# Repacking a 448-row contraction into 128-row chunks with paired 64-row tails

## The chip, the core and the metric

The kernel runs on one core of one Trainium2 chip. The metric is device time in microseconds (us) of one execution. A run is labelled fast or slow; with one core, slow only means over 1.5% above the fastest run of the same kernel. Ratios in this text are the mean time of one kernel's fast runs over the mean of the fast runs of the kernel before from the same rounds, so they are not quite the ratio of the medians quoted beside them. Where a ratio is turned into microseconds it is multiplied by 198.5 us, the median time of the kernel before.

PSUM is the memory into which the matmuls of this kernel write; it is addressed in numbered banks. Engine names in the profile lines: PE is TensorE's matmuls, PEld its weight loads, DVE is VectorE, ACT is ScalarE, POOL is GpSimd. L451 is line 451 of that kernel's own source, so line numbers differ between kernels.

## The reference, cut to what matters

```python
B, S, D, H, F = 1, 2048, 448, 16, 1792          # head size 28; all inputs bf16
xn  = layernorm(x)
q, k, v = split_heads(xn @ wqkv)                 # contraction over D = 448
phi(t)  = concat(softmax(t @ w_phi), softmax(-(t @ w_phi)))
kv, z   = sum_s phi(k)^T v, sum_s phi(k)         # linear attention
o       = (phi(q) @ kv) / (phi(q) @ z + 1e-6)
out     = x + o @ wo + silu(xn @ w1) @ w2        # contractions over 448, 448, 1792
```

## The kernel before

D = 448 is no multiple of 128. The kernel before cuts it into four chunks of 112 rows, so every contraction over D is four matmuls that leave 16 of the 128 rows of the array empty.

A small scheduler in the kernel takes operations with named reads and writes. Each operation waits at its head for everything that it needs, and signals once, after its last instruction. An operation that writes two PSUM banks holds and frees both together.

The feed-forward block, its bank alternating between 6 and 7 (`B_PQ`):

```python
def ffn1_block(b):
    tg, k = divmod(b, NK)
    slot = b % 2
    def f(e):
        for c in range(NC_):                      # 4 chunks of 112 rows
            last = e.matmul(bank(B_PQ[slot])[:, :], lhsT=w1_sb[:, c, k * P:(k + 1) * P],
                            rhs=xnT_sb[:, c, tg * TG:(tg + 1) * TG], start=(c == 0), stop=(c == NC_ - 1))
        return last
    sch.add("pe", f, reads=[...], writes=["bank:%d" % B_PQ[slot]], ...)
    sch.add("act", ... Silu from bank(B_PQ[slot]) into hT_sb ...)
```

There are two stages.

```python
for t in range(NT):            # stage one, 16 tiles of 128 positions
    ...                        # layernorm of a later tile (VectorE, GpSimd)
    kv_proj(t)                 # two operations: keys into bank 1 or 2, values into bank 3
    k_exps(t); v_evac(t)       # ScalarE: two exponentials, value eviction
    k_norm(t)                  # VectorE sums and reciprocals, GpSimd product
    q_block(t)                 # one query block of 512 columns, banks 6 and 7 in turn
    xn_transpose(t + LA)       # 4 transposes
    kv_acc(t - 1)              # 8 small matmuls

while ...:                     # stage two, one iteration:
    ffn1_block x 4             # 16 matmuls of 512 columns
    a_mm, a_combine            # attention matmuls, then VectorE
    o_transpose                # 4 transposes
    final_mm, final_out        # 14 + 4 matmuls of 448 columns into bank 3 or 4, then the output
```

The softmax here doesn't subtract the row's maximum and nothing guards it: scores larger than these inputs give would overflow.

## Time and profile before

The median was 198.54 us in three runs.

| | before |
|---|---|
| span of the profiled execution | 197.3 us |
| first feed-forward matmul (end of stage one) | 79.5 us |
| one steady iteration of stage two | 7.51 us |
| 16 feed-forward matmuls of an iteration | 3.46 us |

From the page of the kernel before: the span, the engines' busy time with its share of the span and the number of instructions, then TensorE's busy tenths and the clock that the throttle granted it, in tenths of full speed, in 40 equal slices.

```profile
span 197.3 us, 2897 instructions
PE 174.9 (89%) x1152; PEld 97.2 (49%) x1152; DVE 106.8 (54%) x227; ACT 90.2 (46%) x156; POOL 34.1 (17%) x35
...
PE   0349696996999994999999999999999999999994
...
PEclk9999999999999999699999999999999999999999
```

TensorE is busy without a break in stage two (from slice 16 on) and has gaps in stage one. By this view its clock falls in one slice, just after a gap of 2.5 us at the end of stage one. Stage two begins here:

```profile
79.50 5.11 PE L553 MATMUL ps<-xnT_sb,w_sb 112*128 112x512 bf16 x16
```

One steady iteration, from the timeline of the kernel before (columns: start in us, length in us, engine, line, operation, output and inputs, count, idle time before it and what ended that):

```profile
119.74 2.81 PE L634 MATMUL ps<-w_sb,hT_sb 128*128 128x448 bf16 x14
...
122.39 0.92 PE L637 MATMUL ps<-wo_sb,EqT_sb 112*128 112x448 bf16 x4
...
123.15 3.62 PE L553 MATMUL ps<-xnT_sb,w_sb 112*128 112x512 bf16 x16
...
126.61 0.58 PE L570 MATMUL ps<-rhs_sb,EqT_sb 112*128 112x120 bf16 x8
...
127.03 0.39 PE L612 MATMUL ps<-ident_sb,o_sb 128*112 128x128 bf16 x4
...
127.25 2.81 PE L634 MATMUL ps<-w_sb,hT_sb 128*128 128x448 bf16 x14
```

Read the starts, not the lengths: records of pipelined matmuls overlap. Sixteen feed-forward matmuls go from 123.15 to 126.61, so one every 216 ns. Nothing waits. The next line, of the waits of weight loads (total us, times, longest us), shows how little the Silu evictions hold TensorE up, since one bank is evicted while the other is filled:

```profile
PEld ps L553 <- ACT hT_sb L559: 8.6, 27, 0.4
```

### The profile page before, as it was taken

What the parts mean: (1) busy time and instruction counts of PE and PEld (TensorE: products, weight loads), DVE (VectorE), ACT (ScalarE), POOL (GpSimd) and SP (SyncE); (2) the same over time, 40 slices, a digit from 0 to 9 for tenths busy, and PEclk for the clock granted to TensorE, in tenths of its full rate; (3) what the DMA queues carried; (4) which work ended last, traced back from release to release, by engine and by line L of the source; (5) the groups of instructions that cost most, each with busy time, mean ns of one, the idle gap of its engine ahead of it and who ended that gap; (6) DMA issues with size and microseconds to landing.
All of it is one profiled execution on the core that took longest, in us unless ns stands there. A gap on an engine that the chain in (4) does not pass through costs nothing.

```text
span 197.3 us, 2897 instructions
## 1 busy us (share of the span) xinstructions
PE 174.9 (89%) x1152; PEld 97.2 (49%) x1152; DVE 106.8 (54%) x227; ACT 90.2 (46%) x156; POOL 34.1 (17%) x35
## 2 busy tenths in 40 slices
PE   0349696996999994999999999999999999999994
PEld 0339363553665652455545545445445445555551
DVE  0559796996775452256745345355255255288321
ACT  2308185675778887266524424424415415420200
POOL 3201035545646556000000000000000000000000
PEclk9999999999999999699999999999999999999999
DMA  5938970000000000000000000000000000001001
GB/s 163 331 127 214 283 239 0 0 2 5 0 0 3 0 0 2 0 3 0 0 23 3 23 23 0 28 23 0 23 28 0 23 19 8 23 5 41 27 23 47
DMA packets 9022, 8.70 MB, mean 44 GB/s; under 512 B 880, under 2 KB 8560, under 8 KB 9008
## 3 DMA queue, kind: packets, MB, share of 16 engines
q1 hardware_dynamic: 7616, 7.31, 12.7%
q10 hardware_dynamic: 1392, 1.20, 2.0%
q8 instruction: 9, 0.15, 0.3%
q14 instruction: 5, 0.04, 0.1%
HBM read 6.68 MB, written 1.84 MB: 43 GB/s over the span
## 4 chain that ended last, share of the span: by engine, by line
PE 69%; DVE 3%; POOLq 1%; issue 1%; ACT 1%
PE ps L553 25%; PE ps L634 21%; PE ps L637 6%; PE ps L570 3%; PE ps L443 3%; PE ps L510 3%; PE ps L495 2%; PE ps L451 2%; PE ps L612 2%; DVE xn_sb L409 1%; DVE S_sb L475 1%; POOLq L199 1%; ACT E_sb L461 1%; PE ps L422 1%; DVE R_sb L479 0%
## 5 line engine op out<-in xcount | busy, mean ns | idle before, releaser
L559 ACT ACTIVATE hT_sb<-ps 128x512 bf16<-128x512 f32 x56 | 33.4, 597 | 54.5 <-PE ps L553 54.5
L553 PE MATMUL ps<-xnT_sb,w_sb 112*128 112x512 bf16 x224 | 52.2, 387 | 0.0
L634 PE MATMUL ps<-w_sb,hT_sb 128*128 128x448 bf16 x224 | 45.0, 352 | 0.0
L553 PEld LDWEIGHTS ps<-xnT_sb,w_sb 112*128 112x128 bf16 x224 | 20.0, 100 | 28.3 <-ACT hT_sb L559 8.6
L481 POOL TENSOR_TENSOR phik_sb<-E_sb,R_sb 128x896 bf16<-128x896 f32 x16 | 27.6, 1722 | 28.5 <-DVE R_sb L479 17.7
L634 PEld LDWEIGHTS ps<-w_sb,hT_sb 128*128 128x128 bf16 x224 | 21.3, 98 | 17.9
L583 DVE RECIPROCAL rneg_sb<-ps 128x16 f32<-128x16 f32 x16 | 4.1, 256 | 39.6 <-PE ps L570 39.6
L475 DVE TENSOR_REDUCE S_sb<-E_sb 128x32 f32<-128x896 f32 x16 | 17.3, 1080 | 10.3 <-ACT E_sb L461 10.2
L646 DVE TENSOR_TENSOR y_sb<-ps,x_sb 128x448 bf16<-128x448 f32 x16 | 10.0, 624 | 16.9 <-PE ps L637 16.9
L518 ACT ACTIVATE EqT_sb<-ps 112x512 bf16<-112x512 f32 x32 | 17.4, 594 | 3.4 <-PE ps L510 3.4
L510 PE MATMUL ps<-xnT_sb,wq_sb 112*112 112x512 bf16 x64 | 16.4, 379 | 0.0
L422 PE MATMUL ps<-ident_sb,xn_sb 128*112 128x128 bf16 x64 | 7.5, 261 | 10.1 <-DVE xn_sb L409 9.7
L443 PE MATMUL ps<-wk_sb,xnT_sb 112*128 112x448 bf16 x64 | 15.5, 366 | 0.0
L451 PE MATMUL ps<-wv_sb,xnT_sb 112*128 112x448 bf16 x64 | 15.0, 358 | 0.0
L458 ACT ACTIVATE E_sb<-ps 128x448 f32<-128x448 f32 x16 | 8.7, 544 | 13.3 <-PE ps L443 13.0
L637 PE MATMUL ps<-wo_sb,EqT_sb 112*128 112x448 bf16 x64 | 14.8, 353 | 0.0
L409 DVE TENSOR_SCALAR xn_sb<-x_sb,mv_sb,rstd_sb 128x448 bf16<-128x448 bf16 x16 | 10.4, 667 | 5.3 <-POOL rstd_sb L402 5.3
L619 ACT ACTIVATE EqT_sb<-ps 112x1024 bf16<-112x1024 bf16 x8 | 8.2, 1024 | 11.0 <-PE ps L612 10.8
L422 PEld LDWEIGHTS ps<-ident_sb,xn_sb 128*112 128x112 bf16 x64 | 5.8, 159 | 14.4 <-DVE xn_sb L409 13.9
L391 DVE BATCH_NORM_STATS2 stats_sb<-x_sb 128x6 f32<-128x448 bf16 x16 | 9.6, 597 | 5.6 <-DMA x_sb<-in_A_x_dram 5.6
L495 PE MATMUL ps<-vaug_sb,phik_sb 128*112 128x113 bf16 x128 | 9.7, 218 | 2.5 <-POOL phik_sb L481 2.5
L510 PEld LDWEIGHTS ps<-xnT_sb,wq_sb 112*112 112x112 bf16 x64 | 8.3, 130 | 5.2
(49 smaller groups left out, 160.4 us busy)
## 6 DMA issues: line engine op xcount, KB each, us to landing
w_sb<-in_B_w_dram SPq DMA_DIRECT2D x2, 1568.0 KB, 11.4
x_sb<-in_A_x_dram SPq DMA_DIRECT2D x4, 448.0 KB, 8.1
out_dram<-y_sb SPq DMA_DIRECT2D x16, 112.0 KB, 1.7
hT_sb<-in_A_wqkv_dram ACTq DMA_DIRECT2D x2, 392.0 KB, 6.0
wv_sb<-in_A_wqkv_dram ACTq DMA_DIRECT2D x1, 392.0 KB, 8.4
wo_sb<-in_A_wo_dram SPq DMA_DIRECT2D x1, 392.0 KB, 9.4
wphi_sb<-in_A_w_phi_dram SPq DMA_DIRECT2D x1, 24.5 KB, 5.2
```

The source lines that it names most:

```text
L422: last = e.transpose(out=bank_bf(B_TP)[0:KC, half * 512 + c * P: half * 512 + (c + 1) * P], in_=xn_sb[:, slot, c * KC:(c + 1) * KC], ident ...
L443: last = e.matmul(bank(B_PK[s2])[:, 0:D], lhsT=xnT_sb[:, c, t * P:(t + 1) * P], rhs=wk2_sb[:, c, :], start=(c == 0), stop=(c == NC_ - 1))
L451: last = e.matmul(bank(B_V)[:, 0:D], lhsT=xnT_sb[:, c, t * P:(t + 1) * P], rhs=wv_sb[:, c, :], start=(c == 0), stop=(c == NC_ - 1))
L475: sch.add("dve", lambda e: e.tensor_reduce(out=S_sb[:, s2, :], in_=E_sb[:, s2, :].rearrange("p (g f) -> p g f", f=DH), axis=AX.X, op=ALU.add),
L481: sch.add("pool", lambda e: e.tensor_tensor(out=phik_sb[:, s2, :].rearrange("p (g f) -> p g f", f=DH), in0=E_sb[:, s2, :].rearrange("p (g ...
L495: last = e.matmul(bank(B_KV[sg])[0:KC, j * NV:(j + 1) * NV], lhsT=phik_sb[:, s2, sg * D + j * KC: sg * D + (j + 1) * KC], rhs=vaug_sb[:, s ...
L510: last = e.matmul(bank(B_PQ[slot])[0:KC, :], lhsT=wq2_sb[:, c, j * KC:(j + 1) * KC], rhs=xnT_sb[:, c, tg * TG:(tg + 1) * TG], start=(c == ...
L518: sch.add("act", lambda e, sg=sg: e.activation(out=EqT_sb[:, j, sg, tg * TG:(tg + 1) * TG], in_=bank(B_PQ[slot])[0:KC, :], func=ACTF.Exp, ...
L553: last = e.matmul(bank(B_PQ[slot])[:, :], lhsT=w1_sb[:, c, k * P:(k + 1) * P], rhs=xnT_sb[:, c, tg * TG:(tg + 1) * TG], start=(c == 0), st ...
L559: sch.add("act", lambda e: e.activation(out=hT_sb[:, k, tg * TG:(tg + 1) * TG], in_=bank(B_PQ[slot])[:, :], func=ACTF.Silu), reads=["bank: ...
L634: last = e.matmul(bank(B_ACC[s2])[:, 0:D], lhsT=hT_sb[:, k, t * P:(t + 1) * P], rhs=w2_sb[:, k, :], start=(k == 0), stop=False)
L637: last = e.matmul(bank(B_ACC[s2])[:, 0:D], lhsT=oT_sb[:, c, t * P:(t + 1) * P], rhs=wo_sb[:, c, :], start=False, stop=(c == NC_ - 1))
```

## The change

The intent: cut 448 into three full chunks of 128 rows and a tail of 64. A tail fills half the array's rows, so the tails of two blocks can run at once, one in the upper and one in the lower half. A pair of blocks then takes 3 + 3 + 1 = 7 matmul slots in place of 8. The lower half needs its own copy of the tail rows in partitions 64 to 127, so tail weights are loaded twice, and the tail of every tile is transposed twice, as two 64-column transposes.

The core of the diff (layouts, loads and the query blocks, which are paired in the same way, are cut):

```diff
+        DC = [(0, 128), (128, 128), (256, 128), (384, 64)]
...
+        def tr_chunks(e, src_ap_fn, half):
+            for c in range(NC_):
+                r0, rn = DC[c]
+                outs = [(0, rn)] if c < 3 else [(0, HK), (HK, HK)]     # HK = 64
+                for (po, pn) in outs:
+                    last = e.transpose(out=bank_bf(B_TP)[po:po + pn, ...], in_=src_ap_fn(r0, pn), ...)
...
+        def kv_proj(t):
+            def f(e):
+                mm_full(e, bank(B_PK[s2])[:, 0:D], xl, wkf)            # 3 matmuls of 128 rows
+                mm_full(e, bank(B_V)[:, 0:D], xl, wvf)
+                mm_half(e, bank(B_PK[s2])[:, 0:D], xl, wkf, 0)         # rows 0 to 63
+                return mm_half(e, bank(B_V)[:, 0:D], xl, wvf, HK)      # rows 64 to 127
+            sch.add("pe", f, ..., writes=["bank:%d" % B_PK[s2], "bank:%d" % B_V], ...)
...
-        def ffn1_block(b):
+        def ffn1_pair(b):
+            def f(e):
+                for kk in range(2): mm_full(e, bank(B_PQ[kk])[:, :], ...)
+                for kk in range(2): last = mm_half(e, bank(B_PQ[kk])[:, :], ..., kk * HK)
+                return last
+            sch.add("pe", f, ..., writes=["bank:%d" % B_PQ[0], "bank:%d" % B_PQ[1]], ...)
...
         def final_mm(t):
-                    last = e.matmul(..., lhsT=oT_sb[:, c, ...], rhs=wo_sb[:, c, :], ...)
+                    rn = DC[c][1]
+                    last = e.matmul(..., lhsT=oT_sb[0:rn, c, ...], rhs=wo_sb[0:rn, c, :], ...)
...
-            q_block(t)
+            if t % 2 == 1:
+                q_pair(t - 1)
```

More of the change, by code (lines that the diff above doesn't have):

```diff
@@ L189, in bass_parallel_sum__linear_kernel_hedgehog__dense_activation_silu__prompt_kernel @@
     NA = HPC * (DH + 2)
+    DC = [(0, 128), (128, 128), (256, 128), (384, 64)]
+    HK = 64
     EPS_LN = 1e-5
@@ L206, in bass_parallel_sum__linear_kernel_hedgehog__dense_activation_silu__prompt_kernel @@
         hT_sb = sb("hT_sb", [P, NK, S], BF16)
-        EqT_sb = sb("EqT_sb", [KC, NC_, 2, S], BF16)
+        EqT_sb = sb("EqT_sb", [P, NC_, 2, S], BF16)
         xn_sb = sb("xn_sb", [P, 4, D], BF16)
-        xnT_sb = sb("xnT_sb", [KC, NC_, S], BF16)
-        wv_sb = sb("wv_sb", [KC, NC_, D], BF16)
-        wq2_sb = sb("wq2_sb", [KC, NC_, D], BF16)
-        wk2_sb = sb("wk2_sb", [KC, NC_, D], BF16)
+        xnT_sb = sb("xnT_sb", [P, NC_, S], BF16)
+        wv_sb = sb("wv_sb", [P, NC_, D], BF16)
+        wq2_sb = sb("wq2_sb", [P, NC_, D], BF16)
+        wk2_sb = sb("wk2_sb", [P, NC_, D], BF16)
         wphi_sb = sb("wphi_sb", [KC, NC_, DH], BF16)
@@ L215, in bass_parallel_sum__linear_kernel_hedgehog__dense_activation_silu__prompt_kernel @@
         wbd_sb = sb("wbd_sb", [KC, NC_, HPC, DH], BF16)
-        w1_sb = sb("w1_sb", [KC, NC_, FF], BF16)
+        w1_sb = sb("w1_sb", [P, NC_, FF], BF16)
         w2_sb = sb("w2_sb", [P, NK, D], BF16)
-        wo_sb = sb("wo_sb", [KC, NC_, D], BF16)
+        wo_sb = sb("wo_sb", [P, NC_, D], BF16)
         wqk_sb = hT_sb[0:KC, 0:2, :].rearrange("p a b -> p (a b)")[:, 0:NC_ * 2 * D].rearrange(
@@ L264, in dma, with ld_chunked @@
                     reads=reads, writes=writes, name=name, dma=True, is_out=is_out)
+        def ld_chunked(q, dst, src, reads, res, name):
+            dma(q, dst[:, 0:3, :], src[0:384, :].rearrange("(c p) n -> p c n", p=P),
+                reads=reads, writes=[res + ":a"], name=name + "a")
+            dma(q, dst[0:HK, 3, :], src[384:448, :], reads=reads, writes=[res + ":b"], name=name + "b")
+            dma(q, dst[HK:P, 3, :], src[384:448, :], reads=reads, writes=[res + ":c"], name=name + "c")
         for g in range(4):
@@ L280, in bass_parallel_sum__linear_kernel_hedgehog__dense_activation_silu__prompt_kernel @@
             if g == 2:
-                dma("act", wv_sb[:, :, :],
-                    A_wqkv[:, 2 * D:3 * D].rearrange("(c p) n -> p c n", p=KC),
-                    reads=[], writes=["wv"], name="ld_wv")
+                ld_chunked("act", wv_sb, A_wqkv[:, 2 * D:3 * D], [], "wv", "ld_wv")
         def late_loads():
             gate = ["xnT:2"]
-            dma("sp", w1_sb[:, :, :], B_w1.rearrange("(c p) n -> p c n", p=KC),
-                reads=gate, writes=["w1"], name="ld_w1")
-            dma("sp", wo_sb[:, :, :], A_wo.rearrange("(c p) n -> p c n", p=KC),
-                reads=gate, writes=["wo"], name="ld_wo")
+            ld_chunked("sp", w1_sb, B_w1, gate, "w1", "ld_w1")
+            ld_chunked("sp", wo_sb, A_wo, gate, "wo", "ld_wo")
             dma("sp", w2_sb[:, :, :], B_w2.rearrange("(k p) n -> p k n", p=P),
@@ L364, in fold @@
                         last = None
-                        for c in range(NC_):
-                            last = e.matmul(
-                                bank(bk)[0:KC, c * KC:(c + 1) * KC],
-                                lhsT=wT_sb[:, qk * NC_ + c, i * KC:(i + 1) * KC],
-                                rhs=wbd_sb[:, c, :, :].rearrange("p a b -> p (a b)"),
-                                start=True, stop=True)
+                        r0, rn = DC[i]
+                        outs = [(0, rn)] if i < 3 else [(0, HK), (HK, HK)]
+                        for (po, pn) in outs:
+                            for c in range(NC_):
+                                last = e.matmul(
+                                    bank(bk)[po:po + pn, c * KC:(c + 1) * KC],
+                                    lhsT=wT_sb[:, qk * NC_ + c, r0:r0 + pn],
+                                    rhs=wbd_sb[:, c, :, :].rearrange("p a b -> p (a b)"),
+                                    start=True, stop=True)
                         return last
@@ L375, in emit_wprep_fold @@
                     dst = (wq2_sb if qk == 0 else wk2_sb)[:, i, :]
-                    src = bank(bk)[0:KC, 0:D]
+                    src = bank(bk)[:, 0:D]
                     if qk == 1 or i % 2 == 0:
@@ L414, in ln_apply @@
                 name="xn%d" % t)
+        def tr_chunks(e, src_ap_fn, half):
+            last = None
+            for c in range(NC_):
+                r0, rn = DC[c]
+                outs = [(0, rn)] if c < 3 else [(0, HK), (HK, HK)]
+                for (po, pn) in outs:
+                    last = e.transpose(
+                        out=bank_bf(B_TP)[po:po + pn, half * 512 + c * P: half * 512 + (c + 1) * P],
+                        in_=src_ap_fn(r0, pn), identity=ident_sb[:, :])
+            return last
         def xn_transpose(t):
@@ L418, in xn_transpose @@
             half = t % 2
-            def f(e):
-                last = None
-                for c in range(NC_):
-                    last = e.transpose(
-                        out=bank_bf(B_TP)[0:KC, half * 512 + c * P: half * 512 + (c + 1) * P],
-                        in_=xn_sb[:, slot, c * KC:(c + 1) * KC],
-                        identity=ident_sb[:, :])
-                return last
-            sch.add("pe", f, reads=["xn:%d" % slot, "ident"], writes=["tp:%d" % half],
-                    name="xnT_tr%d" % t)
+            sch.add("pe", lambda e: tr_chunks(e, lambda r0, rn: xn_sb[:, slot, r0:r0 + rn], half),
+                    reads=["xn:%d" % slot, "ident"], writes=["tp:%d" % half], name="xnT_tr%d" % t)
         def xnT_evac(t0):
@@ L433, in f, with mm_full @@
                     out=xnT_sb[:, :, t0 * P:(t0 + 2) * P].rearrange("p c (h q) -> p h c q", h=2),
-                    in_=bank_bf(B_TP)[0:KC, :].rearrange("p (h c q) -> p h c q", h=2, c=NC_))
+                    in_=bank_bf(B_TP)[:, :].rearrange("p (h c q) -> p h c q", h=2, c=NC_))
             sch.add("dve", f, reads=["tp:0", "tp:1"], writes=["xnT:%d" % t0, "xnT:%d" % (t0 + 1)],
                     name="xnT_evac%d" % t0)
+        def mm_full(e, out_ap, lhs_fn, rhs_fn):
+            last = None
+            for c in range(3):
+                last = e.matmul(out_ap, lhsT=lhs_fn(c, 0, P), rhs=rhs_fn(c, 0, P), start=(c == 0), stop=False)
+            return last
@@ L438, in kv_proj, with mm_half @@
+        def mm_half(e, out_ap, lhs_fn, rhs_fn, po):
+            return e.matmul(out_ap, lhsT=lhs_fn(3, po, HK), rhs=rhs_fn(3, po, HK), start=False, stop=True)
         def kv_proj(t):
             s2 = t % 2
-            def fpk(e):
-                last = None
-                for c in range(NC_):
-                    last = e.matmul(bank(B_PK[s2])[:, 0:D], lhsT=xnT_sb[:, c, t * P:(t + 1) * P],
-                                    rhs=wk2_sb[:, c, :], start=(c == 0), stop=(c == NC_ - 1))
-                return last
@@ L446, in kv_proj @@
-            sch.add("pe", fpk, reads=["xnT:%d" % t] + ["w2_1:%d" % i for i in range(NC_)],
-                    writes=["bank:%d" % B_PK[s2]], name="pk%d" % t)
-            def fv(e):
-                last = None
-                for c in range(NC_):
-                    last = e.matmul(bank(B_V)[:, 0:D], lhsT=xnT_sb[:, c, t * P:(t + 1) * P],
-                                    rhs=wv_sb[:, c, :], start=(c == 0), stop=(c == NC_ - 1))
-                return last
-            sch.add("pe", fv, reads=["xnT:%d" % t, "wv"], writes=["bank:%d" % B_V], name="v%d" % t)
+            xl = lambda c, po, pn: xnT_sb[po:po + pn, c, t * P:(t + 1) * P]
@@ new lines, in kv_proj @@
+            wkf = lambda c, po, pn: wk2_sb[po:po + pn, c, :]
+            wvf = lambda c, po, pn: wv_sb[po:po + pn, c, :]
+            def f(e):
[3 more added lines that the diff above has]
+                return mm_half(e, bank(B_V)[:, 0:D], xl, wvf, HK)
+            sch.add("pe", f, reads=["xnT:%d" % t] + ["w2_1:%d" % i for i in range(NC_)] + ["wv:a", "wv:b", "wv:c"],
+                    writes=["bank:%d" % B_PK[s2], "bank:%d" % B_V], name="pkv%d" % t)
@@ L502, in kv_acc, with q_pair @@
                     writes=["bank:4", "bank:5"], name="kv%d" % t)
-        def q_block(b):
-            tg, j = divmod(b, NC_)
-            slot = b % 2
+        def q_pair(b):
+            tg, j0 = divmod(b, NC_)
+            xr = lambda c, po, pn: xnT_sb[po:po + pn, c, tg * TG:(tg + 1) * TG]
             def f(e):
                 last = None
-                for c in range(NC_):
-                    last = e.matmul(bank(B_PQ[slot])[0:KC, :], lhsT=wq2_sb[:, c, j * KC:(j + 1) * KC],
-                                    rhs=xnT_sb[:, c, tg * TG:(tg + 1) * TG],
-                                    start=(c == 0), stop=(c == NC_ - 1))
+                for jj in range(2):
+                    j = j0 + jj
+                    mm_full(e, bank(B_PQ[jj])[0:KC, :],
+                            lambda c, po, pn, j=j: wq2_sb[po:po + pn, c, j * KC:(j + 1) * KC], xr)
+                for jj in range(2):
+                    j = j0 + jj
+                    last = mm_half(e, bank(B_PQ[jj])[0:KC, :],
+                                   lambda c, po, pn, j=j: wq2_sb[po:po + pn, c, j * KC:(j + 1) * KC], xr, jj * HK)
                 return last
@@ L515, in q_block @@
                     + ["w2_0:%d" % i for i in range(NC_)],
-                    writes=["bank:%d" % B_PQ[slot]], name="pq%d" % b)
-            for sg in range(2):
-                sch.add("act", lambda e, sg=sg: e.activation(
-                    out=EqT_sb[:, j, sg, tg * TG:(tg + 1) * TG], in_=bank(B_PQ[slot])[0:KC, :],
-                    func=ACTF.Exp, scale=(1.0 if sg == 0 else -1.0)),
-                    reads=["bank:%d" % B_PQ[slot]],
-                    writes=["EqT:%d:%d:%d" % (j, sg, t) for t in range(tg * TPG, (tg + 1) * TPG)],
-                    name="qexp%d_%d" % (b, sg))
+                    writes=["bank:%d" % B_PQ[0], "bank:%d" % B_PQ[1]], name="pq%d" % b)
+            for jj in range(2):
+                j = j0 + jj
+                for sg in range(2):
+                    sch.add("act", lambda e, sg=sg, j=j, jj=jj: e.activation(
+                        out=EqT_sb[0:KC, j, sg, tg * TG:(tg + 1) * TG], in_=bank(B_PQ[jj])[0:KC, :],
+                        func=ACTF.Exp, scale=(1.0 if sg == 0 else -1.0)),
+                        reads=["bank:%d" % B_PQ[jj]],
+                        writes=["EqT:%d:%d:%d" % (j, sg, t) for t in range(tg * TPG, (tg + 1) * TPG)],
+                        name="qexp%d_%d" % (b + jj, sg))
         def rhs_build():
@@ L545, in bass_parallel_sum__linear_kernel_hedgehog__dense_activation_silu__prompt_kernel @@
         RHS_RES = ["rhs:0:kv", "rhs:0:z", "rhs:1:kv", "rhs:1:z", "rhs:ones"]
-        def ffn1_block(b):
-            tg, k = divmod(b, NK)
-            slot = b % 2
+        def ffn1_pair(b):
+            tg, k0 = divmod(b, NK)
+            xr = lambda c, po, pn: xnT_sb[po:po + pn, c, tg * TG:(tg + 1) * TG]
             def f(e):
                 last = None
-                for c in range(NC_):
-                    last = e.matmul(bank(B_PQ[slot])[:, :], lhsT=w1_sb[:, c, k * P:(k + 1) * P],
-                                    rhs=xnT_sb[:, c, tg * TG:(tg + 1) * TG],
-                                    start=(c == 0), stop=(c == NC_ - 1))
-                return last
-            sch.add("pe", f, reads=["xnT:%d" % t for t in range(tg * TPG, (tg + 1) * TPG)] + ["w1"],
-                    writes=["bank:%d" % B_PQ[slot]], name="ffn1_%d" % b)
-            sch.add("act", lambda e: e.activation(
-                out=hT_sb[:, k, tg * TG:(tg + 1) * TG], in_=bank(B_PQ[slot])[:, :], func=ACTF.Silu),
-                reads=["bank:%d" % B_PQ[slot]],
-                writes=["hT:%d:%d" % (k, tg)] + (["wqk:0", "wqk:1"] if k < 2 else ["wT:%d" % r for r in range(4)] if k < 4 else []),
-                name="silu%d" % b)
@@ new lines, in f @@
+                for kk in range(2):
+                    k = k0 + kk
+                    mm_full(e, bank(B_PQ[kk])[:, :],
+                            lambda c, po, pn, k=k: w1_sb[po:po + pn, c, k * P:(k + 1) * P], xr)
+                for kk in range(2):
+                    k = k0 + kk
+                    last = mm_half(e, bank(B_PQ[kk])[:, :],
+                                   lambda c, po, pn, k=k: w1_sb[po:po + pn, c, k * P:(k + 1) * P], xr, kk * HK)
+                return last
+            sch.add("pe", f, reads=["xnT:%d" % t for t in range(tg * TPG, (tg + 1) * TPG)] + ["w1:a", "w1:b", "w1:c"],
+                    writes=["bank:%d" % B_PQ[0], "bank:%d" % B_PQ[1]], name="ffn1_%d" % b)
@@ L565, in a_mm @@
+            for kk in range(2):
+                k = k0 + kk
+                sch.add("act", lambda e, k=k, kk=kk: e.activation(
+                    out=hT_sb[:, k, tg * TG:(tg + 1) * TG], in_=bank(B_PQ[kk])[:, :], func=ACTF.Silu),
+                    reads=["bank:%d" % B_PQ[kk]],
+                    writes=["hT:%d:%d" % (k, tg)] + (["wqk:0", "wqk:1"] if k < 2 else ["wT:%d" % r for r in range(4)] if k < 4 else []),
+                    name="silu%d" % (b + kk))
         def a_mm(t):
@@ L571, in f @@
                             bank(B_PK[sg])[:, j * NA:(j + 1) * NA],
-                            lhsT=EqT_sb[:, j, sg, t * P:(t + 1) * P],
+                            lhsT=EqT_sb[0:KC, j, sg, t * P:(t + 1) * P],
                             rhs=rhs_sb[:, sg * NC_ + j, :, :].rearrange("p a b -> p (a b)"),
@@ L608, in o_transpose @@
             s2 = t % 2
-            def f(e):
-                last = None
-                for c in range(NC_):
-                    last = e.transpose(
-                        out=bank_bf(B_TP)[0:KC, s2 * 512 + c * P: s2 * 512 + (c + 1) * P],
-                        in_=o_sb[:, s2, c * KC:(c + 1) * KC], identity=ident_sb[:, :])
-                return last
-            sch.add("pe", f, reads=["o:%d" % s2, "ident"], writes=["tp:%d" % s2], name="oT_tr%d" % t)
+            sch.add("pe", lambda e: tr_chunks(e, lambda r0, rn: o_sb[:, s2, r0:r0 + rn], s2),
+                    reads=["o:%d" % s2, "ident"], writes=["tp:%d" % s2], name="oT_tr%d" % t)
         def oT_evac(t0):
@@ L620, in oT_evac @@
                 out=oT_sb[:, :, t0 * P:(t0 + 2) * P].rearrange("p c (h q) -> p h c q", h=2),
-                in_=bank_bf(B_TP)[0:KC, :].rearrange("p (h c q) -> p h c q", h=2, c=NC_),
+                in_=bank_bf(B_TP)[:, :].rearrange("p (h c q) -> p h c q", h=2, c=NC_),
                 func=ACTF.Copy),
@@ L636, in f @@
                 for c in range(NC_):
-                    last = e.matmul(bank(B_ACC[s2])[:, 0:D], lhsT=oT_sb[:, c, t * P:(t + 1) * P],
-                                    rhs=wo_sb[:, c, :], start=False, stop=(c == NC_ - 1))
+                    rn = DC[c][1]
+                    last = e.matmul(bank(B_ACC[s2])[:, 0:D], lhsT=oT_sb[0:rn, c, t * P:(t + 1) * P],
+                                    rhs=wo_sb[0:rn, c, :], start=False, stop=(c == NC_ - 1))
                 return last
-            sch.add("pe", f, reads=["hT:%d:%d" % (k, tg) for k in range(NK)] + ["w2", "wo", "oT:%d" % t],
+            sch.add("pe", f, reads=["hT:%d:%d" % (k, tg) for k in range(NK)] + ["w2", "oT:%d" % t] + ["wo:a", "wo:b", "wo:c"],
                     writes=["bank:%d" % B_ACC[s2]], name="final%d" % t)
@@ L709, in bass_parallel_sum__linear_kernel_hedgehog__dense_activation_silu__prompt_kernel @@
         while nf < NTG * NK or na < NT or no < NT or nfin < NT:
-            for _ in range(4):
+            for _ in range(2):
                 if nf < NTG * NK:
-                    ffn1_block(nf)
-                    nf += 1
+                    ffn1_pair(nf)
+                    nf += 2
             if na < NT:
```

## The prediction

> **What bounds the kernel now.** TensorE, in two stages. The busy-time windows show TensorE 10.0 of 10 us in nearly every window from 80 to 190 us (feed-forward and output stage), but only 7.5 to 10 in the key/value stage (22 to 79 us), where VectorE (about 8 of 10 us from 30 to 50) and ScalarE (8.7 of 10 from 60 to 70) are close limits. In the timeline one iteration of the second stage takes 7.51 us (119.74 to 127.25): 18 output matmuls 3.4 us, four feed-forward blocks (16 matmuls of 512 columns) 3.46, attention matmuls and transposes 0.65. Matmuls issue every 216 ns (512 columns) and 187 to 188 ns (448), though each record lasts 387 or 352 ns. The waits view shows weight loads waiting for the Silu eviction 27 times, never over 0.4 us: the two banks alternate, one block computing while the other is evicted.
>
> **Removed.** Seven issue slots per pair instead of eight, if the two 64-row tails run at once in different halves of the array. 28 feed-forward pairs x 0.216 = 6.0 us, 8 query pairs x 0.216 = 1.7, 16 key/value pairs x 0.187 = 3.0: 10.8 us at most. The output matmul keeps its 18 slots, since its 64-row tail has no partner.
>
> **Added.**
> 1. A pair writes both banks and signals once, at its end. So the second pair of each iteration must wait for both Silus of the first. From the trace: matmul end to eviction start 0.04 us, two back-to-back evictions 1.09 (as the two query exponentials), release and weight load 0.2, lost overlap of the pipelined records 0.17: an estimated 1.5 us stall, 14 times = 21 us. The pair that opens an iteration is covered by output matmuls, except in the first three iterations, where only 0.6 us of work lies between: another 2 us.
> 2. Mode switches. The Trainium skill (TensorEngine Tiling (Array Packing), Key Properties) says that changing the tiling mode drains TensorE. Nothing in the trace before shows its price; the lost overlap, 387 - 216 = 171 ns, is my upper estimate. Some seven switches per iteration (pairs, output tail, 64-column transposes), part hidden in the stall: I take 0.3 us per iteration, 4 us in all.
> 3. In the first stage key and value projections finish together, so the key exponentials start about 0.55 us later, the next tile waits for the value eviction, and four query exponentials come in one batch. PE savings there meet ScalarE and VectorE as limits; I expect the stage 3 us longer, not 4.7 shorter.
> 4. Setup: 40 fold matmuls instead of 32, 5 transposes instead of 4 per tile, split loads: under 1 us net.
>
> **On the critical path.** Nearly all the second stage is. Per iteration: 7.51 + 1.5 - 0.43 + 0.3 = 8.9 us. Stage two +21 us, stage one and setup +3.5: 198.5 + 24.5 = 223 us. Range 211 to 236. Chances: faster 0.04, within 2% 0.04, slower 0.92.
>
> **What would show it.** In the waits view, TensorE waiting on the Silu eviction about 14 to 17 times, 1.2 to 1.6 us each (step 1 right); iteration period near 8.9 us; the two tail matmuls of a pair starting within about 20 ns (packing works) or 216 ns apart (it doesn't); gaps beyond the normal spacing around tail matmuls without a semaphore wait (drains); first feed-forward matmul later than 79.5 us.
>
> **What would make it wrong.** Tails that serialise (+10 us); a drain far above or below my guess; the clock: it fell after the 2.5 us idle at 76 to 79 us, and repeated stalls could trigger it again; weight loads of 128 instead of 112 columns making transposes cheaper than thought; a stall shortened because Silus overlap more than the query exponentials.

## The result

The changed kernel is correct and took 238.43 us in the median of 12 runs (234.25 to 239.18). The ratio of the fast runs is 1.193, with a 95% interval of 1.188 to 1.198, or about 38 us more. That is slower, as predicted, but above the stated range of 211 to 236. Seven of the 12 runs carry the label slow; the mean of the five fast ones is 236.4 us, so by fast runs alone it lies only just above the range.

The same views of the changed kernel. The profiled execution carries the label slow, at 238.44 us. What sets such runs apart isn't shown: their mean granted clocks (0.964 to 0.978) overlap those of the fast ones (0.969 to 0.985). The steady iteration below is therefore taken from a stretch where the granted clock was 1.00.

```profile
span 236.7 us, 2956 instructions
PE 189.8 (80%) x1182; PEld 90.8 (38%) x1192; DVE 106.4 (45%) x227; ACT 86.4 (37%) x156; POOL 33.7 (14%) x35
...
PE   0466869969988985677879798798798797899995
...
PEclk9999797997999997699999999999999999999999
```

TensorE now has gaps all through stage two, and by this view its clock falls in five slices instead of one (the first of the five is at the first key matmuls, which are as slow in the kernel before). One steady iteration, from the timeline:

```profile
154.65 2.82 PE L654 MATMUL ps<-w_sb,hT_sb 128*128 128x448 bf16 x14
...
157.31 1.02 PE L658 MATMUL ps<-wo_sb,EqT_sb 128*128 128x448 bf16 x4
...
158.26 1.47 PE L451 MATMUL ps<-xnT_sb,w_sb 128*128 128x512 bf16 x6
...
159.66 0.39 PE L455 MATMUL ps<-xnT_sb,w_sb 64*128 64x512 bf16 x2
160.09 1.09 ACT L585 ACTIVATE hT_sb<-ps 128x512 bf16<-128x512 f32 x2 [4.98 <-PE ps L455]
...
161.23 1.47 PE L451 MATMUL ps<-xnT_sb,w_sb 128*128 128x512 bf16 x6 [1.18 <-ACT hT_sb L585]
...
162.63 0.39 PE L455 MATMUL ps<-xnT_sb,w_sb 64*128 64x512 bf16 x2
162.96 0.59 PE L596 MATMUL ps<-rhs_sb,EqT_sb 112*128 112x120 bf16 x8
...
163.39 0.51 PE L429 MATMUL ps<-ident_sb,o_sb 128*128 128x128 bf16 x5
...
163.83 2.82 PE L654 MATMUL ps<-w_sb,hT_sb 128*128 128x448 bf16 x14
```

The iteration is 163.83 - 154.65 = 9.18 us, against 7.51. Four things can be read off.

- The first pair ends, ScalarE runs two Silus back to back (1.09 us), and only then does the second pair start, at 161.23.
- Packing works. Two tails together have a record of 0.39 us, the length of one matmul. The Trainium skill, TensorE: Matmul & The Clock Gate, Part 3, gives about 4 ns between the starts of neighbouring row tiles (drawn there for tiles of 32 rows). Here the key and value tails start 0 to 10 ns apart, which agrees as far as a trace printed in steps of 10 ns can tell.
- It isn't free. Six full matmuls starting at 161.23 would let the next one start at 161.23 + 6 x 0.216 = 162.53; the tails start at 162.63, 0.10 us late. The next operation starts at 162.96, 0.33 after the tails and not 0.216, so 0.11 us late again. The pair takes 162.96 - 161.23 = 1.73 us; two blocks took 3.46 / 2 = 1.73 us before.
- The output matmul's four chunks take 158.26 - 157.31 = 0.95 us (0.76 before), and the transposes 0.44 us (0.22 before).

The Trainium skill, TensorEngine Tiling (Array Packing), Key Properties, says that changing the tiling mode drains TensorE, without a figure. This trace fits that, with 0.10 us lost on the way in and 0.11 us on the way out. The same page's Gotcha 1 (PSUM Pressure) says that row tiles write to different PSUM banks. The first point follows: a packed pair here holds both of the stage's two banks until its end, and nothing is left to fill while they are evicted.

The waits of TensorE in the changed kernel (total us, times, longest us):

```profile
PE ps L451 <- ACT hT_sb L585: 19.2, 17, 1.6
PE ps L429 <- DVE xn_sb L416: 10.6, 6, 2.8
...
PE ps L509 <- POOL phik_sb L495: 3.9, 4, 2.4
PE ps L451 <- ACT vaug_sb L481: 2.5, 5, 0.8
```

The first line is the predicted stall: 17 times. Each wait is counted from the end of a record; the lost overlap of about 0.17 us that the prediction names comes on top.

Stage one also grew. Its end, the first feed-forward matmul:

```profile
91.63 2.24 PE L451 MATMUL ps<-xnT_sb,w_sb 128*128 128x512 bf16 x5
```

That is 91.6 against 79.5 us, 12.1 us later, where the prediction had 3.5 with setup. From there to the end it is 236.7 - 91.6 = 145.1 against 117.8 us, 27.3 more, where the prediction had 21. (Both are from the one slow profile; the fast runs are some 2 us shorter in all.)

### The profile page after: what moved, and what is told of

The parts are those of the page before. It is cut to its first block, busy times and chain, and to the rows that moved or that the text cites. A ratio compares the mean times of both kernels' runs of the same rounds, so it can differ in the third digit from the quotient of the medians.

```text
span 236.7 us, 2956 instructions
## 1 busy us (share of the span) xinstructions
PE 189.8 (80%) x1182; PEld 90.8 (38%) x1192; DVE 106.4 (45%) x227; ACT 86.4 (37%) x156; POOL 33.7 (14%) x35
## 3 DMA queue, kind: packets, MB, share of 16 engines
q10 hardware_dynamic: 1488, 1.26, 1.8%
## 4 chain that ended last, share of the span: by engine, by line
PE 57%; ACT 12%; issue 3%; DVE 2%; POOL 1%; POOLq 1%; ACTq 0%
PE ps L451 22%; PE ps L654 19%; ACT hT_sb L585 8%; PE ps L658 6%; PE ps L455 5%; PE ps L596 3%; PE ps L429 2%; POOL phik_sb L495 1%; DVE S_sb L489 1%; ACT EqT_sb L538 1%; ACT E_sb L475 1%; ACT vaug_sb L481 1%; POOLq L201 1%; ACT E_sb L472 1%; PE ps L509 1%
## 5 line engine op out<-in xcount | busy, mean ns | idle before, releaser
L451 PE MATMUL ps<-xnT_sb,w_sb 128*128 128x512 bf16 x158 | 41.8, 397 | 19.8 <-ACT hT_sb L585 19.2
L451 PEld LDWEIGHTS ps<-xnT_sb,w_sb 128*128 128x128 bf16 x168 | 14.6, 100 | 39.6 <-ACT hT_sb L585 23.3
L429 PE MATMUL ps<-ident_sb,xn_sb 128*128 128x128 bf16 (+1 forms) x80 | 9.2, 255 | 10.6 <-DVE xn_sb L416 10.6
L658 PE MATMUL ps<-wo_sb,EqT_sb 128*128 128x448 bf16 x64 | 16.4, 354 | 0.0
L451 PE MATMUL ps<-wk_sb,xnT_sb 128*128 128x448 bf16 x48 | 13.1, 386 | 2.7 <-ACT vaug_sb L481 2.5
L451 PE MATMUL ps<-wv_sb,xnT_sb 128*128 128x448 bf16 x48 | 13.5, 395 | 0.0
L451 PE MATMUL ps<-xnT_sb,wq_sb 128*112 128x512 bf16 x48 | 12.6, 401 | 0.0
L639 ACT ACTIVATE EqT_sb<-ps 128x1024 bf16<-128x1024 bf16 x8 | 8.2, 1028 | 11.8 <-PE ps L429 11.8
L455 PE MATMUL ps<-xnT_sb,w_sb 64*128 64x512 bf16 x56 | 11.2, 396 | 0.0
L429 PEld LDWEIGHTS ps<-ident_sb,xn_sb 128*128 128x128 bf16 (+1 forms) x80 | 4.9, 108 | 16.1 <-DVE xn_sb L416 12.5
## 6 DMA issues: line engine op xcount, KB each, us to landing
w_sb<-in_B_w_dram SPq DMA_DIRECT2D x1, 1568.0 KB, 12.1
```

What stands on the lines that cost most here:

```text
L429: last = e.transpose(out=bank_bf(B_TP)[po:po + pn, half * 512 + c * P: half * 512 + (c + 1) * P], in_=src_ap_fn(r0, pn), identity=ident_sb ...
L451: last = e.matmul(out_ap, lhsT=lhs_fn(c, 0, P), rhs=rhs_fn(c, 0, P), start=(c == 0), stop=False)
L455: return e.matmul(out_ap, lhsT=lhs_fn(3, po, HK), rhs=rhs_fn(3, po, HK), start=False, stop=True)
L658: last = e.matmul(bank(B_ACC[s2])[:, 0:D], lhsT=oT_sb[0:rn, c, t * P:(t + 1) * P], rhs=wo_sb[0:rn, c, :], start=False, stop=(c == NC_ - 1))
```

## The experiments

Theories: grouping (paired operations that wait and signal together), mode switches, and the granted clock. Every kernel gave a correct result.

### Stall of the feed-forward pairs, taken away and alone

e1_four_banks, from the changed kernel:

```diff
+            BF = ((6, 7), (4, 5))[(b // 2) % 2]
-                    mm_full(e, bank(B_PQ[kk])[:, :], ...        # tails and Silus likewise
+                    mm_full(e, bank(BF[kk])[:, :], ...
+                acc = 3 if nf < NTG * NK else B_ACC[t % 2]      # the output keeps to bank 3 meanwhile
```

> The changed kernel with the feed-forward pairs alternating between two pairs of PSUM banks (6,7 and 4,5), so that no pair waits for its own predecessor's Silus; the output accumulator keeps to one bank while the feed-forward part runs. Stall theory: the 17 waits on the Silu eviction (19.2 us in the waits view of the changed kernel) vanish, steady iteration 9.18 -> about 7.9 us, time about 237 -> 219 (216 to 222). Rival (mode switches cost most of the time, the wait only covers a drain that is due anyway): the gain is under 8 us.

Measured: 216.06 us (four runs, two of them slow), ratio 1.083, at the low edge of what was expected. The wait on the Silus is gone from the list of TensorE's waits. The steady iteration, from the timeline, is 166.09 - 158.15 = 7.94 us:

```profile
158.15 2.82 PE L654 MATMUL ps<-w_sb,hT_sb 128*128 128x448 bf16 x14
...
166.09 2.82 PE L654 MATMUL ps<-w_sb,hT_sb 128*128 128x448 bf16 x14
```

e2_ffn_sync_only, from the kernel before:

```diff
-                    writes=["bank:%d" % B_PQ[slot]], name="ffn1_%d" % b)
+                    writes=["bank:%d" % B_PQ[0], "bank:%d" % B_PQ[1]], name="ffn1_%d" % b)   # f does two blocks
```

> The kernel before, 112-row chunks and no tiling, with nothing changed but that two feed-forward blocks are one operation that writes both banks and signals once. Stall theory: about +18 us (14 stalls near 1.3 us, three more of about 0.6 to 0.8 us), iteration 7.51 -> about 8.8. Rival (the switches are the cost): 198.5 us, within 2 us.

Measured: 220.27 us, ratio 1.110, with no tiling in the kernel at all. Its waits:

```profile
PE ps L554 <- ACT hT_sb L562: 19.0, 17, 1.3
```

Its steady iteration is 130.87 - 122.01 = 8.86 us:

```profile
122.01 2.81 PE L637 MATMUL ps<-w_sb,hT_sb 128*128 128x448 bf16 x14
...
130.87 2.81 PE L637 MATMUL ps<-w_sb,hT_sb 128*128 128x448 bf16 x14
```

The two runs agree from both sides. Taking the stall away gives back (1.1930 - 1.0829) x 198.5 = 21.9 us; adding it alone costs 0.1103 x 198.5 = 21.9 us. Each is uncertain by about 2 us, so that they agree to the tenth is luck. Most of that sum is in the waits line: 19.0 us, plus an estimated 17 x 0.17 us of lost overlap, is 21.9. The expectation of +18 us was low, but its own terms (14 x 1.3 + 3 x 0.7) add to 20.3, and the iteration is close to its 8.8 us.

### What packing earns, and what the switches cost

e3_pad_ffn, from the changed kernel, packs nothing in the feed-forward part:

```diff
+        sch.add("pool", lambda e: e.memset(w1_sb[:, 3, :], 0.0), ...)     # lower half of the tail chunk stays zero
-                    last = mm_half(e, bank(B_PQ[kk])[:, :], ..., kk * HK)
+                    last = e.matmul(bank(B_PQ[kk])[:, :], lhsT=w1_sb[:, 3, k * P:(k + 1) * P],
+                                    rhs=xr(3, 0, P), start=False, stop=True)
```

> The changed kernel with the feed-forward tails not packed: each tail is a 128-row matmul against a chunk whose lower 64 weight rows are zero, so 8 full-mode matmuls per pair, no mode switch there. Theory that the two switches (0.10 us in, 0.11 us out, read from the trace) eat the slot that packing saves (0.216 us): time unchanged within 2 us, steady iteration 9.18 within 0.1 (out-switch of the first pair is hidden in the stall, so up to 0.1 longer). Rival (packing gains its 28 x 0.216 = 6 us and the loss is elsewhere): +6 us.

Measured: 240.05 us, ratio 1.202 (1.190 to 1.214), beside 1.193 (1.188 to 1.198) with packing. The intervals overlap; the difference is 1.8 us, uncertain by about 2.6, and not the 6 us of the rival. The timeline shows why:

```profile
155.09 1.47 PE L455 MATMUL ps<-xnT_sb,w_sb 128*128 128x512 bf16 x6 [1.32 <-ACT hT_sb L589]
156.40 0.59 PE L582 MATMUL ps<-xnT_sb,w_sb 128*128 128x512 bf16 x2
156.83 0.58 PE L600 MATMUL ps<-rhs_sb,EqT_sb 112*128 112x120 bf16 x8
```

Eight full matmuls take 156.83 - 155.09 = 1.74 us. Seven slots with two switches took 1.73. That is for a pair with matmuls right behind it. The steady iteration without packing is 9.29 us (148.26 - 138.97), 0.11 more than the 9.18 with it: where a stall follows the pair, the switch out is hidden in the stall, as the expectation allowed. Over 17 stalls that is 1.9 us in favour of packing, about what was measured.

e4_out_no_switch, from the changed kernel, takes the switches out of the output path:

```diff
-        o_sb = sb("o_sb", [P, 2, D], BF16)
+        o_sb = sb("o_sb", [P, 2, 512], BF16)                 # columns 448 to 511 zero
-                    ... tr_chunks(...)                        # 3 transposes and 2 of 64 columns
+                    ... 4 transposes of 128 columns
-                    rn = DC[c][1]; ... lhsT=oT_sb[0:rn, c, ...], rhs=wo_sb[0:rn, c, :]
+                    ... lhsT=oT_sb[:, c, ...], rhs=wo_sb[:, c, :]
```

> The changed kernel with the output path free of mode switches: the attention output tile is widened with zero columns, so 4 full transposes instead of 3 plus 2 of 64 columns, and the output matmul's tail runs over 128 rows (the added ones zero). Switch theory: per tile 0.44 -> about 0.22 us for the transposes and 0.20 us less around the tail, 16 times each: 5 to 7 us less, iteration 9.18 -> about 8.77. Rival (these gaps are hidden or have another cause): no change, within 1.5 us.

Measured: 229.45 us, ratio 1.155, so (1.1930 - 1.1547) x 198.5 = 7.6 us less, a little more than expected. The timeline:

```profile
161.10 0.39 PE L640 MATMUL ps<-ident_sb,o_sb 128*128 128x128 bf16 x4
161.33 2.81 PE L663 MATMUL ps<-w_sb,hT_sb 128*128 128x448 bf16 x14
163.97 0.92 PE L666 MATMUL ps<-wo_sb,EqT_sb 128*128 128x448 bf16 x4
164.73 1.46 PE L453 MATMUL ps<-xnT_sb,w_sb 128*128 128x512 bf16 x6
...
170.07 2.81 PE L663 MATMUL ps<-w_sb,hT_sb 128*128 128x448 bf16 x14
```

The transposes are back at 0.23 us and the tail chunks at 0.76; the iteration is 8.74 us instead of 9.18. The edit also removes the fifth transpose of each tile, by an estimate from these lines 16 x 0.055 = 0.9 us, so not all of the 7.6 is switches.

### Stage one

e5_stage1_sync_only, from the kernel before:

```diff
-            sch.add("pe", fpk, ..., writes=["bank:%d" % B_PK[s2]], ...)
-            sch.add("pe", fv, ..., writes=["bank:%d" % B_V], ...)
+            sch.add("pe", f, ..., writes=["bank:%d" % B_PK[s2], "bank:%d" % B_V], ...)     # keys, then values
-            q_block(t)
+            if t % 2 == 1:
+                q_block(t - 1)                                # two blocks, both banks, one signal
```

> The kernel before with only the grouping of the key/value stage taken from the change: key and value projection as one operation with one signal, query blocks two at a time; 112-row chunks, no tiling. The changed kernel reaches its first feed-forward matmul at 91.6 us against 79.5. If the grouping (later key exponentials, wait for the value eviction, query exponentials in one batch) is the cause of that: first feed-forward matmul 6 to 10 us later, 204 to 208 us in all. If the mode switches or the clock are: within 2 us of the kernel before.

Measured: 209.66 us, ratio 1.0546 or 10.8 us, more than expected. Stage one ends 11 us later than before, at 90.5 us, almost as late as in the changed kernel, with no mode switch in it:

```profile
90.54 5.30 PE L552 MATMUL ps<-xnT_sb,w_sb 112*128 112x512 bf16 x16
```

e6_split_kv, from the changed kernel, splits the key and value pair into four operations in the same order:

```diff
+            sch.add("pe", ... mm_full keys ...,   writes=["bank:%d" % B_PK[s2]])
+            sch.add("pe", ... mm_full values ..., writes=["bank:%d" % B_V])
+            sch.add("pe", ... mm_half keys ...,   writes=["bank:%d" % B_PK[s2]])
+            sch.add("pe", ... mm_half values ..., writes=["bank:%d" % B_V])
```

> The changed kernel with the key/value pair split into four operations, so that the key matmuls no longer wait for the value eviction of the tile before and the key exponentials start a little earlier. The waits view of the changed kernel has 2.5 us for that wait. Theory that the shared wait costs: 2 to 4 us less, first feed-forward matmul 2 to 4 us earlier. Rival (the wait only moves to the value matmuls, since ScalarE and VectorE set the period): within 1.5 us.

Measured: 234.12 us, ratio 1.1765 or 3.3 us less. The first feed-forward matmul is at 89.98 us, 1.7 us earlier and not 2 to 4, but the two profiles differ in how the clock fell there, so the total is the better guide. The shared wait costs something; it is not most of stage one's loss.

e7_warm, from the changed kernel:

```diff
+            if t in (2, 6):
+                keep_warm(B_PK[1 - t % 2], 8)      # 8 full matmuls into a free bank, result never read
             if t + LA < NT:
                 xn_transpose(t + LA)
...
+        keep_warm(B_PK[0], 9)
         kv_acc(NT - 1)
```

> The changed kernel with dummy matmuls (results never read) in three idle gaps of TensorE: 8 in the gap of 2.2 us at the third and seventh tile, 9 in the gap of 2.4 us before the last key/value accumulation. Clock theory: the granted clock no longer falls after them (slices at 0.7 vanish), 3 to 6 us less. Rival (the lower clock is hidden behind ScalarE and VectorE, or doesn't come from the gaps): within 1 us, or slower by the dummies.

Measured: 232.65 us, ratio 1.1723 or 4.1 us less. The clock now falls in one slice, early, after a gap of 2.04 us in which nothing was added:

```profile
PEclk9999799999999999999999999999999999999999
```

What happens without the dummies, from the timeline of the changed kernel at the third tile:

```profile
35.84 0.52 PE L429 MATMUL ps<-ident_sb,xn_sb 128*128 128x128 bf16 x5 [2.19 <-DVE xn_sb L416]
...
36.74 0.96 PE L451 MATMUL ps<-wk_sb,xnT_sb 128*128 128x448 bf16 x3
37.50 1.33 PE L451 MATMUL ps<-wv_sb,xnT_sb 128*128 128x448 bf16 x3
```

After a gap of 2.19 us the three value matmuls take 38.76 - 37.50 = 1.26 us instead of the usual 0.66 (as from 32.62 to 33.28 in the tile before). In the kernel before the gap at the same tile is 1.74 us, and the clock holds:

```profile
33.58 0.43 PE L422 MATMUL ps<-ident_sb,xn_sb 128*112 128x128 bf16 x4 [1.74 <-DVE xn_sb L409]
```

The cause of the gap is the same in both, a wait for the layernorm of a later tile. But in the kernel before a query block runs ahead of the transpose in every tile; pairing moved the query work to every second tile (the second, the fourth and so on), and this wait falls on the third and the seventh.

The length of the gap alone doesn't decide it. In the kept profiles of kernels with paired queries and no dummies at these two tiles, the clock fell there in all 14 cases (gaps of 1.69 to 2.47 us); with a query block in every tile it fell in one of 12 (1.53 to 1.77 us; the one, in e2, was 1.75). Before the last accumulation it fell after seven gaps of 2.07 to 2.59 us and held after five of 2.17 to 2.53. What else decides was not tested.

### Do the parts add up?

e8_sync_all is the kernel before with the edits of e2 and e5 together.

> The kernel before with both groupings and no tiling at all: feed-forward blocks, query blocks and key with value in pairs, one signal each, 112-row chunks. If the parts add: 198.5 + 22 (feed-forward grouping) + 11 (key/value stage grouping) = 231.5 us, 229 to 234; the changed kernel is then some 6 us slower still, by its mode switches less its saved slots. If the two groupings overlap in what they cost: under 227. If the whole change is grouping: 237.

Measured: 229.75 us, ratio 1.1558 or 30.9 us (its fast runs; the profiled one was slow). The parts alone are 21.9 + 10.8 = 32.7, so they add within 2 us. The changed kernel is (1.1930 - 1.1558) x 198.5 = 7.4 us slower still, and e4 found 7.6 us in the output path.

### A version that keeps the idea

b1_group4 keeps 128-row chunks and packs only the feed-forward tails, four blocks at a time in banks 4 to 7, so that two switches serve two packed pairs, and the evictions of the group run under the output matmuls. Stage one is synchronised as before, its tails padded to 128 rows with zeros, and all transposes in the steady loop have 128 columns.

```diff
+        def ffn1_group(b, banks):                       # one operation per block, one per packed pair of tails
+            for q in range(n): sch.add("pe", ... mm_full(e, bank(banks[q])[:, :], ...), writes=[that bank])
+            for h in range(0, n, 2): sch.add("pe", ... two mm_half ..., writes=[both banks])
+            for q in range(n): sch.add("act", ... Silu ...)
+        def dup_tail(tg):                               # upper half of the tail chunk, copied by DMA
+            dma("sp", xnT_sb[HK:P, 3, ...], xnT_sb[0:HK, 3, ...], ...)
...
+            if nf < GRP_FROM * 4:  ffn1_group(nf, (6, 7)); ffn1_group(nf + 2, (4, 5))    # GRP_FROM = 3
+            else:                  ffn1_group(nf, (6, 7, 4, 5))
```

(A group that would cross a 512-column boundary also goes as two pairs.)

> An attempt at a version that keeps the idea and beats both: 128-row chunks, but the first stage synchronised as before with its tails zero-padded to 128 rows, all transposes of 128 columns, the output tail padded; only the feed-forward tails are packed, four blocks to a group (12 full matmuls, then two packed pairs) in four PSUM banks, the duplicate rows for the upper half copied by DMA. From the traces: per iteration 14 x 0.216 + 0.21 = 3.23 us for the feed-forward part against 3.46, in about 9 iterations: 2 us less than before, 194 to 198 us. If groups of four stall on the Silus after all: over 200.

Measured: 194.90 us, ratio 0.980 (0.975 to 0.985). One iteration from the timeline:

```profile
103.02 2.81 PE L673 MATMUL ps<-w_sb,hT_sb 128*128 128x448 bf16 x14
...
106.42 2.75 PE L464 MATMUL ps<-xnT_sb,w_sb 128*128 128x512 bf16 x11
109.11 0.61 PE L474 MATMUL ps<-xnT_sb,w_sb 64*128 64x512 bf16 x4
109.64 0.59 PE L609 MATMUL ps<-rhs_sb,EqT_sb 112*128 112x120 bf16 x8
...
110.30 2.81 PE L673 MATMUL ps<-w_sb,hT_sb 128*128 128x448 bf16 x14
```

(One of the 12 full matmuls has no record.) The feed-forward part takes 109.64 - 106.42 = 3.22 us against 3.46, and the iteration 7.28 us against 7.51.

Three further runs tell what earned that. The first sets GRP_FROM to 14, so that every group is two pairs in alternating bank pairs:

> The four-block version with its groups taken apart into pairs in alternating bank pairs, all else equal. Two switches per pair cost 0.21 us and the packing saves 0.216, so against the kernel before the feed-forward part is even: about 10 iterations x 0.22 = 2.2 us slower than the groups of four, so 0.989 of the kernel before or a little more. Rival (the gain of the four-block version has nothing to do with packing, but with the 128-column transposes or the clock): the same time as the groups of four within 0.7 us.

> The four-block version once more, unchanged, beside its pair version on one chip, to give the 2% of its first run an interval of under half a per cent: 0.980 of the kernel before, 0.975 to 0.985.

> The four-block version with 9 dummy matmuls in the gap of 2.2 us before the last key/value accumulation. If the clock falls there in some executions: granted clock 1.0 in all, 0 to 1.5 us less and less scatter. If it doesn't in this version (its profile shows 1.0): no change, or 0.2 us more.

The pairs took 196.16 us, ratio 0.989 (0.985 to 0.993); the groups, on the same chip, 194.32 us, ratio 0.979 (0.976 to 0.982). So grouping four blocks earns 1.8 us, which is the packing gain that survives once two switches are spread over two packed pairs. In the pairs kernel an iteration is 109.09 - 101.60 = 7.49 us, even with the 7.51 before: packing pair by pair, without a stall, is worth nothing.

```profile
101.60 2.81 PE L673 MATMUL ps<-w_sb,hT_sb 128*128 128x448 bf16 x14
...
109.09 2.81 PE L673 MATMUL ps<-w_sb,hT_sb 128*128 128x448 bf16 x14
```

The 2 us between the pairs kernel and the kernel before lie outside the steady iteration (stage one ends at 78.2 us in its profile, and the clock doesn't fall just after); which edit earned them was not tested. Nine dummies before the last accumulation (b2_group4_warm) changed nothing: 194.49 us, ratio 0.981. The four-block version is faster than both kernels, but at 2.1% it can't be said with confidence to be over 2% faster.

## Why the prediction was wrong

| term | predicted | measured | by |
|---|---|---|---|
| stall of feed-forward pairs | +23 us (21 + 2) | +21.9 | e1, e2 |
| slots saved, feed-forward | -6.0 us | -6.0, mostly cancelled by the pairs' own switches in the row below | trace, e3 |
| mode switches, all of stage two | +4 us | about +4 around the pairs (5.9 less 1.9 hidden), +7.6 in the output path | trace, e3, e4 |
| stage one with setup | +3.5 us | +12.1 in the profile, 10.8 by grouping alone | e5 |

**The stall (added, step 1) was right** in mechanism, count (17 times) and total. A single one was nearer 1.35 us (1.18 in the record plus 0.17) than 1.5, and the three early ones (0.80, 0.54 and 0.31 in the record) came on top as expected.

**The packing (removed) was right in kind**: the two tails do run at once. Their slot was saved, and paid for again by the switches around it, except where a stall hid one of them.

**Mode switches (added, step 2) failed in size.** The text took 0.3 us per iteration for seven switches, with 171 ns each as an upper estimate. They cost 0.10 us in and 0.11 us out: about 0.21 for each pair, 0.19 for the output tail and 0.22 for the transposes, hidden only where a stall follows. With 28 pairs that is 28 x 0.21 = 5.9 us in the feed-forward part, less 17 x 0.11 = 1.9 us hidden in the stalls, and 7.6 us in the output path (with the fifth transpose), so between 11 and 12 us against 4. Had the text applied its own upper estimate to each switch without a hidden part, it would have seen that two of them outweigh the slot of 0.216 us that a pair saves.

**Stage one (added, step 3) failed in size by a factor of three.** The direction was right: later exponentials, the wait for the value eviction, queries in a batch. Two things were missed. The query work left the third and seventh tile, so the gap there grew past 2 us and the clock fell after it; dummies there and at the stage's end gave back 4.1 us (uncertain by about 2). The text named the clock as a risk but gave it no time. And the stage has too little slack: over its last six tiles a tile took (84.61 - 63.49) / 6 = 3.52 us instead of (73.19 - 55.79) / 6 = 2.90, measured from key matmul to key matmul. How the 10.8 us split between those two was not separated further; the shared wait on the value eviction accounts for about 3 us (e6).

**Setup (step 4)** was not tested alone; the first key matmul starts 1.1 us later (23.41 against 22.35), a little over the "under 1 us" of the text.

Together: the stall was met within about 1 us, the switches were 7 to 8 us more than forecast, and stage one 7 to 9. The measured terms, 21.9 - 6.0 + 4.0 + 7.6 + 10.8, add to the 38.3 us of the fast runs; given the uncertainty of each, and that e8 fell 2 us short of its own two parts, so close a sum is partly luck. The median lay 15 us above the point and 2 above the range, the fast runs 13 above the point.

## What to carry to other kernels

When work is merged to share a resource, count the buffers first: a pair that fills both of two buffers and signals once removes the double-buffering, and here that alone cost 11% with no other change. A saving of one slot has to be set against the cost of entering and leaving the mode that saves it; here they cancelled at one packed pair per visit, unless a stall hid one of the two switches, and without stalls packing paid only at two pairs per visit. And work that moves off a stretch where an engine would otherwise wait lengthens that wait, which can cost the clock as well.

## What the Trainium skill lacked or had wrong

- TensorEngine Tiling (Array Packing), Key Properties: says that a mode change drains TensorE, but not what that costs. Here, with matmuls of 512 columns, 0.10 us on entering a 64-row mode and 0.11 us on leaving it; two 64-column transposes in place of one full one cost 0.22 us per tile (0.44 against 0.22), the extra transpose included. It lacks a warning that one packed pair of 512 columns (0.216 us saved) does no more than pay for its two switches.
- TensorEngine Tiling (Array Packing), Performance Considerations: names PSUM eviction as what may become the bottleneck, and Gotcha 1 the pressure on banks, but not the loss of double-buffering when a packed pair takes all the banks of a stage: 21.9 us of 198.5 here.
- TensorE: Matmul & The Clock Gate, "Why this matters for your kernels": advises against gaps of TensorE over about 3 us. In these runs the clock also fell after shorter gaps (2.19 us in the changed kernel, 1.69 in e3, 1.75 in e2), though not after every gap of that length (it held after 2.53 in e2); filling three gaps with dummies gave 4.1 us.
